# Three edits in a fused attention, MoE and routed-MoE kernel: one head first, dots by a count per step, a first gather without the last tile

## The chip, the cores and the metric

The kernel runs on one core of a Trainium2 chip. The core has five engines that each run their own queue of instructions: TensorE for matmuls (PE in the rows; PEld is its weight load), VectorE (DVE), ScalarE (ACT), GpSimd (POOL) and SyncE (SP), which here only issues transfers. Data lie in SBUF, matmul results in PSUM, inputs and outputs in HBM, and DMA engines move data between them. The metric is the time of one execution on the device in microseconds (us); lower is better.

## The reference

Three stages follow one another, each on the result of the one before. x has 1152 tokens of 512 numbers after the attention.

```python
def _attn_ref(q, k, v):                 # B 2, H 8, S 576, D 64
    q_rot, k_rot = (rotate(q), rotate(k))        # halves mixed with cos and sin of the position
    scores = scale * np.matmul(q_rot, k_rot.transpose(0, 1, 3, 2))
    scores = scores - np.max(scores, axis=-1, keepdims=True)
    attn = np.exp(scores)
    attn = attn / (np.sum(attn, axis=-1, keepdims=True) + 1e-09)
    return np.matmul(attn, v)

def _moe_ref(x, w_gate, w1, w2):        # N 1152, D 512, E 8, F 1024
    logits = x @ w_gate
    logits = logits - logits.max()
    P = np.exp(logits)
    for _ in range(8):
        P /= P.sum(1, keepdims=True) + 1e-09
        P /= P.sum(0, keepdims=True) + 1e-09
        P *= N / E
    for e in range(E):
        h = np.maximum(x @ w1[e], 0.0)
        out += P[:, e:e + 1] * (h @ w2[e])

def _moe2_ref(x, w_gate, w1, w2):       # same sizes, other weights
    logits = x @ w_gate
    order = np.argsort(-logits.flatten())
    for idx in order:                    # best pair of token and expert first
        tok, e = (int(idx) // E, int(idx) % E)
        if assigned[tok] >= 0 or counts[e] >= N // E:
            continue
        assigned[tok] = e
        counts[e] += 1
    for e in range(E):
        mask = assigned == e
        out[mask] = np.maximum(x[mask] @ w1[e], 0.0) @ w2[e]
```

## The kernel before

All matrices are fp32. Where a product needs full precision, an operand is split into a high part and a low part (ACT writes the high part, DVE or POOL subtracts it for the low part), and PE multiplies the parts.

**Attention** goes over 16 heads, two of them a pair P (variable g for the head; h is its place in the pair). For a pair, k and q are loaded (`load`, L1147), rotated (`prep_rot`, L1196, into `t1k` and `t1q`), split (`prep_hl`, L1211, into `hlk` and `hlq`) and transposed by PE (`tq`, L1242, into `khh`, `kll`, `qs`); v is split by `prep_v`. Then five tiles of scores per head follow: matmuls `S`, maximum, exponential, transposes of the result (`te`), product with v. Pair 0 is prepared ahead of the first score as a whole, both heads, and POOL rotates pair 1 meanwhile. What else falls into a head is placed by numbers: `at(2.9, ...)` puts a call behind 2.9 of its five tiles. Between them PE runs dummy matmuls (`warm`) at the start.

**The first MoE** (class Moe1) takes the experts one after the other; six of them by Strassen's scheme, expert 7 plainly in 24 steps (`step`, steps counted from K7). In each step PE makes a block of h, ACT writes its high part (L690), DVE its low part (L691), and the products with w2 add up in PSUM and are added to `acc` (nine tiles of 128 tokens). The gate of the second MoE is folded into this stage: its logits need 72 dot products (nine tiles by eight experts) of `acc` with the gate's columns `g2`, each one DVE instruction (`dot`, L966), and small matmuls (L1020, L1031) for what expert 7 adds. `plan` (L968) puts the dots into the steps: four a step from K7+3, three a step from K7+15. Weights come as raw tiles; `wconv` (L591) splits them, the low part on POOL (L607).

**The second MoE** (`moe2`) is written by a list scheduler (class Plan, L121): each operation has the operations it needs, an engine with an estimated duration, and a function; the planner emits them in order of estimated start, and PE's expert matmuls are its main line. For each expert a phase p picks tokens: `m` and its broadcast, compares (L229 to L232) on DVE, counts on PE (L241), `ok`, `a` and closing on DVE, the selection (`selb`, L297), its place (L302, L304), a one-hot matrix `hot` (L313), the row numbers (L320 on PE, `ix` L328 on DVE). With these POOL gathers the tokens' rows from `ysc` in HBM by two indirect transfers (L338, `xa` and `xb`), PE transposes them (L413, L414) and runs the matmuls of the expert (L422 with w1, L432 with w2, L441 back).

The seam is where the two stages meet. The last products of expert 7 for tiles 3 to 8 (the tail) fill PE while phase 0 picks its tokens. A finished tile of `acc` is written to `ysc` by `save` (L961) from SP's queue. The first gather waits for all saves, that of the last tile (8) among them. Behind the tail PE runs 24 dummy matmuls (`fill`, L484) until the gathered rows are there.

## Time and profile before

| | |
|---|---|
| Time, median of three runs | 1177.39 us (1174.03 to 1178.0) |
| Profiled execution, its own time | 1178.97 us |
| Its span (first to last instruction) | 1177.2 us |
| PE busy | 1148.8 us, 98% |
| DVE busy | 817.9 us, 69% |
| ACT busy | 421.4 us, 36% |
| POOL busy | 500.6 us, 43% |

One core's execution is shown. The profiled time lies 1.8 us above its span, and 1.6 us above the median. PE is nearly always busy, so the rows to read are the few in which it is not, and those in which what it does is a dummy: `warm` at the start, `fill` at the seam. In a row of the timeline the first number is the start in us, the second the length of the instruction (or of the group, with its count behind x), and the bracket at the end says how long the engine had been idle before it and what ended that. A wait for several things is put down to the one that came last.

### The profile page before, as it was taken

How to read it: one execution, taken by the hardware profiler on the slowest of the kernel's cores; microseconds unless marked ns; L12 is line 12 of the kernel's file. 1: busy time of each engine (PE TensorE's matmuls, PEld its weight loads, DVE VectorE, ACT ScalarE, POOL GpSimd, SP SyncE). 2: the span in 40 equal slices, each digit the busy share in tenths (PEclk: the TensorE clock that was granted, in tenths of full speed). 3: DMA queues.
4: the chain of work that ended last, by engine and by line, in shares of the span. 5: the costliest groups of instructions: out<-in, count | busy, mean ns of one | idle time of the engine just before them, and what ended most of it. 6: DMA issues, size and time to landing. Idle time of an engine off the chain costs nothing. (4 is left out here: it accounts for less than half of the span.)

```text
span 1177.2 us, 20269 instructions
## 1 busy us (share of the span) xinstructions
PE 1148.8 (98%) x7788; PEld 1029.8 (87%) x7791; DVE 817.9 (69%) x1785; ACT 421.4 (36%) x966; POOL 500.6 (43%) x460
## 2 busy tenths in 40 slices
PE   7999999999999999999999999999999999999997
PEld 4998988898888889888888889898989877899997
DVE  5999995256477777777777777666667888889200
ACT  4888886214322323232322232323322110222222
POOL 6787865405453434443453435433433000374111
PEclk9999999999999999999999999999999999999999
DMA  3223214200123222423233222111212003878830
GB/s 105 74 61 95 58 34 144 78 1 1 54 71 106 84 90 74 132 82 90 81 111 105 77 86 81 45 36 37 69 58 89 28 1 126 296 262 289 270 101 21
DMA packets 105247, 108.97 MB, mean 93 GB/s; under 512 B 27584, under 2 KB 68672, under 8 KB 105024
## 3 DMA queue, kind: packets, MB, share of 16 engines
q1 hardware_dynamic: 102816, 102.31, 28.0%
q0 software_dynamic: 2048, 4.72, 1.3%
q8 instruction: 61, 1.00, 0.4%
q10 hardware_dynamic: 288, 0.66, 0.2%
q14 instruction: 34, 0.28, 0.1%
HBM read 98.36 MB, written 4.72 MB: 88 GB/s over the span
## 5 line engine op out<-in xcount | busy, mean ns | idle before, releaser
L925 DVE SCALAR_TENSOR_TENSOR acc<-Y,pw,acc 128x512 f32<-128x512 f32 x216 | 158.5, 743 | 3.6 <-PE Y L923 2.6
L861 PE MATMUL T<-xH,wa 128*128 128x256 f32 (+1 forms) x576 | 137.6, 294 | 1.6 <-ACT v L881 1.3
L861 PEld LDWEIGHTS T<-big,wb 128*128 128x128 f32 x864 | 125.9, 188 | 12.6 <-DVE v L874 3.5
L861 PE MATMUL T<-big,wb 128*128 128x256 f32 (+1 forms) x864 | 133.9, 297 | 1.2 <-DVE v L874 1.2
L874 DVE TENSOR_TENSOR v<-T,v 128x256 f32<-128x256 f32 (+1 forms) x240 | 108.3, 451 | 37.4 <-PE T L861 34.5
L861 PEld LDWEIGHTS T<-xH,wa 128*128 128x128 f32 x576 | 99.9, 188 | 9.8 <-ACT v L881 4.1
L770 POOL TENSOR_TENSOR wa<-wraw,wa 128x512 fp32r<-128x512 f32 (+1 forms) x48 | 48.9, 1018 | 108.2 <-ACT wa L769 108.2
L682 PE MATMUL T<-xH,wa 128*128 128x384 f32 x336 | 92.7, 337 | 0.0
L867 ACT ACTIVATE hhA<-v 128x256 fp32r<-128x256 f32 x72 | 30.1, 418 | 152.6 <-DVE v L874 152.6
L861 PE MATMUL T<-xL,wa 128*128 128x256 f32 (+1 forms) x288 | 84.5, 293 | 0.0
L868 DVE SCALAR_TENSOR_TENSOR hlB<-v,hhB 128x320 fp32r<-128x320 f32 x72 | 56.9, 790 | 38.7 <-ACT hhB L867 38.7
L867 ACT ACTIVATE hhB<-v 128x320 fp32r<-128x320 f32 x72 | 34.0, 472 | 138.4 <-DVE v L874 138.4
L993 DVE SCALAR_TENSOR_TENSOR fr<-fr,fc 128x512 f32<-128x512 f32 x64 | 52.5, 820 | 34.4 <-DMA fr<-in_moe_w 34.4
L923 PE MATMUL Y<-wb,hhB 128*128 128x512 f32 x240 | 75.1, 394 | 0.0
L868 DVE SCALAR_TENSOR_TENSOR hlA<-v,hhA 128x256 fp32r<-128x256 f32 x72 | 50.6, 702 | 35.3 <-ACT hhA L867 35.3
L923 PE MATMUL Y<-wa,hhB 128*128 128x512 f32 x240 | 75.0, 394 | 0.0
L789 POOL TENSOR_TENSOR wb<-wraw,wb 128x512 fp32r<-128x512 f32 x24 | 30.6, 1297 | 103.4 <-ACT wb L788 103.4
L789 POOL TENSOR_TENSOR wa<-wraw,wa 128x512 fp32r<-128x512 f32 x24 | 30.6, 1297 | 99.9 <-ACT wa L788 99.9
L701 PE MATMUL Y<-wb,hh 128*128 128x512 f32 x216 | 69.0, 400 | 1.6 <-ACT acc L708 1.6
L1284 DVE TENSOR_REDUCE negmax<-S 128x1 f32<-128x576 f32 (+1 forms) x80 | 60.0, 751 | 6.8 <-PE S L1282 6.0
L682 PEld LDWEIGHTS T<-xH,wa 128*128 128x128 f32 x336 | 61.3, 188 | 2.0
L1288 ACT ACTIVATE big<-S,negmax 128x576 f32<-128x576 f32 (+1 forms) x80 | 59.0, 737 | 11.3 <-DVE negmax L1284 10.7
(294 smaller groups left out, 2995.6 us busy)
## 6 DMA issues: line engine op xcount, KB each, us to landing
wraw<-in_moe_w SPq DMA_DIRECT2D x52, 512.0 KB, 5.3
fr<-in_moe_w SPq DMA_DIRECT2D x64, 256.0 KB, 4.9
wraw<-in_moe_w SPq DMA_DIRECT2D x48, 256.0 KB, 3.2
big<-in_moe_w SPq DMA_DIRECT2D x20, 512.0 KB, 6.2
wa<-in_moe_w SPq DMA_DIRECT2D x18, 512.0 KB, 5.2
wb<-in_moe_w SPq DMA_DIRECT2D x14, 512.0 KB, 6.8
hlk<-hlk SPq DMA_DIRECT2D x14, 320.0 KB, 3.7
ysc<-acc SPq DMA_DIRECT2D x9, 256.0 KB, 2.1
```

Source lines behind the costliest of these rows:

```text
L682: nc.tensor.matmul(p[:, :CH], w[:, wi, kt, (fb % 2) * 128:(fb % 2) * 128 + 128], x[:, kt, o], start=(n == 0), stop=(n == 11))
L701: nc.tensor.matmul(self.Y[c][t], a[:, o], w[:, wi, fb % 2], start=(fb == 0 and n == 0), stop=(fb == FB - 1 and n == 2))
L789: G.tensor_tensor(d["W"][:, 1, h], r[:, 2 + h], d["W"][:, 0, h].bitcast(F32), op=OP.subtract)
L861: nc.tensor.matmul(bank[:, 0:n], d[t][:, ww, b, r * 128:(r + 1) * 128], x(xw, r), start=(first and i == 0), stop=(i == 5), skip_group_chec ...
L867: A.activation(HH[:, f, o], src, AF.Relu)
L868: V.scalar_tensor_tensor(HL[:, f, o], src, 0.0, HH[:, f, o].bitcast(F32), op0=OP.max, op1=OP.subtract)
L874: V.tensor_tensor(o, bank[:, 0:n], x, op=OP.add)
L923: nc.tensor.matmul(y, h[:, f, o], w[:, ww, f], start=(f == 0 and z == 0), stop=(f == 1 and z == 2))
L925: V.scalar_tensor_tensor(self.acc[:, t], y, self.pw[:, t, e:e + 1], self.acc[:, t], op0=OP.mult, op1=OP.add)
L993: nc.vector.scalar_tensor_tensor(r, r, 1.0, self.fc, op0=OP.mult, op1=OP.mult, accum_out=self.wf[:, f, e:e + 1])
L1284: nc.vector.tensor_reduce(m[0:n], p[0:n, :, :288], axis=AX.XY, op=OP.max, negate=True)
L1288: pexp.append(lambda: nc.scalar.activation(e[0:n, :576].rearrange("p (a c) -> p a c", a=2), p[0:n, :, :288], AF.Exp, bias=m[0:n], scale=1. ...
```

## The change

It has three parts.

**Attention.** Only head 0 is prepared ahead of the first score. `prep_rot` and `prep_hl` take a head of the pair as an argument, and `prep_rot` an engine. k of head 0 is rotated by DVE, q of head 0 by POOL; then POOL rotates k of head 1 and k of pair 1. q of head 1 is rotated by DVE within head 0, and its low parts and those of k's head 1 are made there. The loads are issued in that order, k and q have two raw buffers, the table of cosines and sines is loaded once and scaled for q by ACT. The split of k of pair 1 moves from 0.9 to 2.9 of head 0, behind v, the rotation of its q behind that, and the split of its q to 1.6 of head 1.

**Dots.** `plan` now has a list with the number of dots for each of the 24 steps of expert 7: from its first step on, five at most, two in the last five. The first ones go by gate columns that lie in tiles of the fold (`FC`) before `g2` is there. Six low parts of weights in the steps 0, 1 and 3 go to DVE instead of POOL.

**Seam.** The fills are gone. The first gather waits for the saves of tiles 3 to 7 only (they go by ACT's queue now), and the last tile's rows of `ysc` are zeroed beforehand (`zero`); their part of expert 0's input is added afterwards by four matmuls with the one-hot matrix and two additions on DVE (`late`). Behind the gathers of experts 0 and 1 POOL sets a word, which DVE copies (`tock`): DVE stops there until the gather is issued. The save of tile 8 goes behind the first gather.

The order in which POOL's instructions stand at the start of attention, before (names ending in k, q and v are those of k, q and v; `hlk` and `hlq` the low parts):

```order
L1205 TENSOR_TENSOR t_139<-rawq_95,tab 128x10x32
L1206 TENSOR_TENSOR t_139<-rawq_95,tab 128x10x32
L1205 TENSOR_TENSOR t_207<-rawk_96,tab 128x10x32
L1206 TENSOR_TENSOR t_207<-rawk_96,tab 128x10x32
L1208 TENSOR_TENSOR t1k<-rawk_96,tab 128x640
L1209 TENSOR_TENSOR t1k<-t1k,t_207 128x640
L1205 TENSOR_TENSOR t_213<-rawq_95,tab 128x10x32
L1206 TENSOR_TENSOR t_213<-rawq_95,tab 128x10x32
L1208 TENSOR_TENSOR t1q<-rawq_95,tab 128x640
L1209 TENSOR_TENSOR t1q<-t1q,t_213 128x640
L1222 TENSOR_TENSOR hlk<-t1k,hlk 128x10x64
L1234 TENSOR_TENSOR big_113<-rawv_97,zero 128x2x5x64
```

and after:

```order
L1243 TENSOR_TENSOR t2k<-rawk_97,tab 128x5x32
L1244 TENSOR_TENSOR t2k<-rawk_97,tab 128x5x32
L1248 TENSOR_TENSOR t1k<-rawk_97,tab 128x320
L1249 TENSOR_TENSOR t1k<-t1k,t2k 128x320
L1243 TENSOR_TENSOR t2k<-rawk_98,tab 128x10x32
L1244 TENSOR_TENSOR t2k<-rawk_98,tab 128x10x32
L1248 TENSOR_TENSOR t1k<-rawk_98,tab 128x640
L1249 TENSOR_TENSOR t1k<-t1k,t2k 128x640
L1278 TENSOR_TENSOR big_123<-rawv_99,zero 128x2x5x64
L1279 TENSOR_TENSOR big_123<-rawv_99,big_123 128x2x5x64
L1263 TENSOR_TENSOR hlk<-t1k,hlk 128x10x64
L1243 TENSOR_TENSOR t2q<-rawq_96,tab 128x10x32
```

Pieces of 320 (one head) stand ahead of pieces of 640, k of pair 1 stands before v, and q of pair 1 last, where it stood ahead of v.

DVE in the last steps of expert 7, before (L691 is the low part of h, L966 the dots):

```order
L966 SCALAR_TENSOR_TENSOR junk,lg<-acc,g_9447 128x512 x3
L691 SCALAR_TENSOR_TENSOR wraw<-T,wraw 128x384
L966 SCALAR_TENSOR_TENSOR junk,lg<-acc,g_9447 128x512 x3
L691 SCALAR_TENSOR_TENSOR wraw<-T,wraw 128x384
L966 SCALAR_TENSOR_TENSOR junk,lg<-acc,g_9447 128x512 x3
```

and after (L707 and L984):

```order
L707 SCALAR_TENSOR_TENSOR wraw<-T,wraw 128x384
L984 SCALAR_TENSOR_TENSOR junk,lg<-acc,g_9476 128x512 x2
L707 SCALAR_TENSOR_TENSOR wraw<-T,wraw 128x384
L984 SCALAR_TENSOR_TENSOR junk,lg<-acc,g_9476 128x512 x2
L707 SCALAR_TENSOR_TENSOR wraw<-T,wraw 128x384
L984 SCALAR_TENSOR_TENSOR junk,lg<-acc,g_9476 128x512 x2
L707 SCALAR_TENSOR_TENSOR wraw<-T,wraw 128x384
```

There are two dots between low parts where there were three.

DVE at the seam, before (the compares of phase 1; L710 adds tile 8):

```order
L229 TENSOR_SCALAR cmp<-mb,m 128x512
L231 TENSOR_SCALAR cmp<-mb,m 128x512
L232 SCALAR_TENSOR_TENSOR cmp<-mb,m,edge 128x128
L229 TENSOR_SCALAR cmp<-mb,m 128x640
L231 TENSOR_SCALAR cmp<-mb,m 128x384
L232 SCALAR_TENSOR_TENSOR cmp<-mb,m,edge 128x128
L710 SCALAR_TENSOR_TENSOR acc<-Y,pw,acc 128x512
```

and after (L341 is the copy that stops DVE; L726 adds tile 8):

```order
L231 TENSOR_SCALAR cmp<-mb,m 128x640
L232 SCALAR_TENSOR_TENSOR cmp<-mb,m,edge 128x128
L341 COPY tock<-tick 1x1
L726 SCALAR_TENSOR_TENSOR acc<-Y,pw,acc 128x512
L229 TENSOR_SCALAR cmp<-mb,m 128x512
L231 TENSOR_SCALAR cmp<-mb,m 128x512
```

The copy and the addition of tile 8 stand two compares (groups of three rows) earlier than that addition did, and the copy right ahead of it.

PE at the seam, from the sum of phase 1 (L256) to its placing (L302), before:

```order
L256 LDWEIGHTS ones_b
L256 MATMUL PV<-a,ones_b 128x72
L484 LDWEIGHTS ones_b
L484 MATMUL Y<-hot,ones_b 128x512
L484 LDWEIGHTS ones_b
L484 MATMUL Y<-hot,ones_b 128x512
L413 MATMUL Y<-ident,xa 128x72
L414 MATMUL Y<-ident,xb 128x72
L413 MATMUL Y<-ident,xa 128x72
L414 MATMUL Y<-ident,xb 128x72
L302 LDWEIGHTS bef_b
L302 MATMUL PV<-selb,bef_b 128x9
```

and after:

```order
L256 LDWEIGHTS ones_b
L256 MATMUL PV<-a,ones_b 128x72
L445 MATMUL Y<-xg,wa 128x144 x8
L302 LDWEIGHTS bef_b
L302 MATMUL PV<-selb,bef_b 128x9
```

Eight of expert 0's first matmuls (L445) now stand ahead of the placing of phase 1, and the transposes of the gathered rows stand earlier, outside this piece. Eight more stand between it and phase 1's index matmuls (L320), where there were two.

The diff, cut to its core:

```diff
             def gather():
...
+                xa = two.tile([HC, D], F32, name="xa")
+                xb = two.tile([HC, D], F32, name="xb")
...
-                if p == 0:
-                    G.memset(tick, 0)
+                if p < 2:
+                    t = tick if p == 0 else two.tile([1, 1], I32, name="tick1", bufs=1)
+                    G.memset(t, 0)
+                    V.tensor_copy(two.tile([1, 1], I32, name="tock"), t)
+
+            def zero():
+                z = two.tile([128, D], F32, name="zero", bufs=1)
+                G.memset(z, 0.0)
+                nc.sync.dma_start(ysc[(NT - 1) * 128:, :], z)
+
+            def hot_last():
+                d["hf"] = two.tile([128, CAP], F32, name="hotf", bufs=1)
+                nc.scalar.activation(d["hf"], d["hot"][:, NT - 1], AF.Copy)
...
-            op("ga", ["ad"] + ([("tin1", p - 2)] if p > 1 else []) + ([("ga", p - 1)] if p else [("save", t) for t in range(3, NT)]),
-               [("POOL", 2.1, 0.0), ("DMA", 0.9, 1.5 if p == 0 else 5.0)], gather)
+            op("ga", ["ad"] + ([("tin1", p - 2)] if p > 1 else []) + ([("ga", p - 1)] if p else ["zero"] + [("save", t) for t in range(3, NT - 1)]) +
+               ([("save", NT - 1)] if p == 1 else []),
+               [("POOL", 2.1, 0.0), ("DMA", 0.9, 5.0)] if p > 1 else [("DVE", 2.5, 0.0), ("DMA", 0.9, 5.0 if p else 1.0)], gather)
...
+            def late(h):
+                pt = m1.ybank()[:, 0:2 * CAP].rearrange("p (k c) -> p k c", k=2)
+                for k in range(2):
+                    o = slice((2 * h + k) * 128, (2 * h + k + 1) * 128)
+                    nc.tensor.matmul(pt[:, k], m1.acc[:, NT - 1, o], d["hf"], start=True, stop=True)
+                x = Z["xg", p][:, 2 * h:2 * h + 2]
+                V.tensor_tensor(x, pt, x, op=OP.add)
...
-        for i in range(CFG["FILL"]):
-            plan.add(("fill", i), [("spr", 0)], [("PE", 0.23, 0.0)], fill, main=True)
...
-        nc.gpsimd.tensor_tensor(l, r, h.bitcast(F32), op=OP.subtract)
+        (low or nc.gpsimd).tensor_tensor(l, r, h.bitcast(F32), op=OP.subtract)
...
-        self.nc.sync.dma_start(self.ysc[t * 128:(t + 1) * 128, :], self.acc[:, t])
+        (self.nc.sync if t < 3 else self.nc.scalar).dma_start(self.ysc[t * 128:(t + 1) * 128, :], self.acc[:, t])
...
-        put(k7 + 3, 4, [f for t in range(3, NT) for f in part(t, self.pl)])
+        p = [part(t, self.pl) for t in range(3, NT)]
+        dots = [q[e] for e in range(E) for q in p] + [f for t in range(3) for f in part(t, self.lg)]
+        for o, n in enumerate((1, 1, 4, 2, 4, 4, 5, 5, 3, 4, 4, 4, 3, 3, 3, 3, 3, 3, 3, 2, 2, 2, 2, 2)):
+            put(k7 + o, n, dots[:n])
+            dots = dots[n:]
         put(k7 + 9, 3, [lambda t=t: self.save(t) for t in range(3)])
-        put(k7 + 15, 3, [f for t in range(3) for f in part(t, self.lg)])
...
                 for part in range(2):
-                    self.wconv(x, part)
+                    self.wconv(x, part, low=self.nc.vector)
...
-        NR = 1
-        WARM = (8, 6, 3, 4, 3, 2, 2)
+        NR = {"q": 2, "k": 2, "v": 1}
+        WARM = (16, 3, 2, 4, 3, 2, 2)
...
-        load(0, "k")
-        nc.scalar.dma_start(tab[:, 1], rope[:, 1])
-        load(0, "q")
-        nc.scalar.dma_start(tab[:, 0], rope[:, 0])
+        nc.scalar.dma_start(tab[:, 1], rope)
+        for n in "kq":
+            load_h(0, n, 0)
+            load_r(0, n)
+        for n in "kq":
+            load_h(0, n, 1)
+        load(1, "k")
         load(0, "v")
+        load(1, "q")
+        nc.scalar.activation(tab[:, 0], tab[:, 1], AF.Copy, scale=0.125)
...
-        prep_rot(0, "k")
-        prep_rot(0, "q")
-        load(1, "kq")
-        prep_hl(0, "k")
-        prep_hl(0, "q")
+        prep_rot(0, "k", 0, nc.vector)
+        prep_rot(0, "q", 0)
+        prep_hl(0, "k", 0)
+        prep_rot(0, "k", 1)
+        prep_rot(1, "k")
+        prep_hl(0, "q", 0)
...
             if g == 0:
-                at(0.9, prep_hl, 1, "k")
-                at(0.9, load, 2, "kq")
+                at(0.02, prep_rot, 0, "q", 1, nc.vector)
+                at(0.9, prep_hl, 0, "k", 1)
+                at(1.3, prep_hl, 0, "q", 1)
                 at(1.9, prep_v, 0)
                 at(1.9, load, 1, "v")
-                at(2.9, prep_hl, 1, "q")
+                at(2.9, prep_hl, 1, "k")
+                at(2.91, prep_rot, 1, "q")
+                at(2.91, load, 2, "kq")
+            if g == 1:
+                at(1.6, prep_hl, 1, "q")
```

## Rows read from the trace of the kernel before

**Rows 1.** Page, part 2: busy tenths of PE in 40 slices.

```profile
PE   7999999999999999999999999999999999999997
```

**Rows 2.** Waits of PE: us in total, times, longest.

```profile
PE T L1242 <- ACT hlk L1227: 5.5, 1, 5.5
...
PE PV L1020 <- DVE wraw L691: 1.6, 1, 1.6
```

**Rows 3.** Timeline of PE in attention: start, length, operation, idle before.

```profile
18.00 1.04 PE L1280 MATMUL S<-khh,qs 128*128 128x288 f32 x2
...
35.71 0.60 PE L1242 MATMUL T<-ident,hlq 128*128 128x128 f32 x4
```

**Rows 4.** Timeline of DVE, start of attention.

```profile
6.32 0.49 DVE L1205 TENSOR_TENSOR t<-rawk,tab 128x320 f32<-128x320 f32 x1 [4.59 <-DMA rawk<-in_k]
...
12.60 1.48 DVE L1228 TENSOR_TENSOR hlk<-t1k,hlk 128x640 fp32r<-128x640 f32 x1
```

**Rows 5.** DMA issues of 0:9: count, KB each, median us to landing.

```profile
rawk<-in_k SPq DMA_DIRECT2D x2, 32.0 KB, 3.4
```

**Rows 6.** Timeline of POOL, start of attention.

```profile
14.77 2.12 POOL L1208 TENSOR_TENSOR t1k<-rawk,tab 128x640 f32<-128x640 f32 x1
...
18.57 0.85 POOL L1205 TENSOR_TENSOR t<-rawq,tab 128x320 f32<-128x320 f32 x1
...
21.84 1.55 POOL L1209 TENSOR_TENSOR t1q<-t1q,t 128x640 f32<-128x640 f32 x1
```

**Rows 7.** Timeline of ACT, head 0 of attention.

```profile
28.05 0.73 ACT L1221 ACTIVATE hlq<-t1q 128x640 fp32r<-128x640 f32 x1
```

**Rows 8.** Windows: length, busy us of PE, PEld, DVE, ACT, POOL; clock.

```profile
20.00:30.00 10.00, 9.31 (x68) 6.92 (x66) 7.71 (x13) 8.09 (x20) 8.71 (x7) 1.00 0.43 109
880.00:890.00 10.00, 10.00 (x53) 9.20 (x52) 1.87 (x3) 3.02 (x5) 5.06 (x3) 1.00 0.84 315
```

**Rows 9.** Timeline of DVE, late steps of expert 7.

```profile
946.54 0.68 DVE L966 SCALAR_TENSOR_TENSOR junk<-acc,g 128x512 f32<-128x512 f32 x1
...
961.66 0.55 DVE L691 SCALAR_TENSOR_TENSOR wraw<-T,wraw 128x384 fp32r<-128x384 f32 x1
```

**Rows 10.** Timeline of ACT, last step of expert 7.

```profile
959.78 0.49 ACT L690 ACTIVATE wraw<-T 128x384 fp32r<-128x384 f32 x1 [1.89 <-PE T L682]
```

**Rows 11.** Timeline of PE, end of expert 7.

```profile
962.27 0.34 PE L1020 MATMUL PV<-wraw,wfs 128*16 128x384 f32 x1 [1.60 <-DVE wraw L691]
...
964.92 2.15 PE L209 MATMUL T<-ident,m 128*128 128x128 f32 x9
```

**Rows 12.** Window behind the end of expert 7, columns as above.

```profile
964.00:970.00 6.00, 6.00 (x24) 4.99 (x24) 4.12 (x15) 1.47 (x3) 0.00 (x0) 0.72 0.00 0
```

**Rows 13.** Timeline of POOL at the seam: gathers of experts 0 and 1.

```profile
1001.07 1.15 POOL L338 DMA_INDIRECT xa<-ysc,ix  x1 [17.38 <-DVE cmp L229]
1002.52 0.96 POOL L338 DMA_INDIRECT xb<-ysc,ix  x1 [0.31 <-issue]
...
1012.63 6.88 POOL L338 DMA_INDIRECT xb<-ysc,ix  x1 [0.30 <-issue]
```

**Rows 14.** Timeline of DVE at the seam.

```profile
991.28 0.16 DVE L328 SCALAR_TENSOR_TENSOR ix<-idf 72x4 int32<-72x4 f32 x1
...
994.27 0.34 DVE L232 SCALAR_TENSOR_TENSOR cmp<-mb,m,edge 128x128 bf16<-128x128 f32 x1
...
997.29 0.75 DVE L710 SCALAR_TENSOR_TENSOR acc<-Y,pw,acc 128x512 f32<-128x512 f32 x1 [0.58 <-PE Y L701]
...
1005.11 0.18 DVE L297 CAST selb<-sel 128x9 bf16<-128x9 f32 x1
```

**Rows 15.** Page, part 6: the saves of acc to ysc.

```profile
ysc<-acc SPq DMA_DIRECT2D x9, 256.0 KB, 2.1
```

**Rows 16.** Timeline of PE at the seam.

```profile
1008.01 0.79 PE L320 MATMUL PV<-meta,hot 128*72 128x4 bf16 x18 [0.26 <-DVE hot L313]
```

**Rows 17.** Chain that ended last: h matmuls of a later expert.

```profile
1103.60 6.13 PE Y L422 x50
```

More of the change, by code (lines that the diff above doesn't have):

```diff
@@ L370, in phase @@
             if not last:
+                if p == 0:
+                    op("zero", [], [("POOL", 0.7, 0.1), ("SP", 0.1, 0.0), ("DMA", 0.9, 1.6)], zero)
+                    op("hf", ["spr"], [("ACT", 0.3, 0.1)], hot_last)
                 op("m", [("close", p - 1), ("left", p - 1)] + ([("at", p)] if p == 1 else []) if p else [], [("DVE", 0.5, 0.15)], prefer)
@@ L408, in tin @@
                 if h == 0:
-                    Z["xg", p] = X["p"].tile([128, KT, CAP], F32, name="xg")
+                    Z["xg", p] = two.tile([128, KT, CAP], F32, name="xg")
                 pt = m1.ybank()[:, 0:2 * CAP].rearrange("p (k c) -> p k c", k=2)
@@ L459, in expert @@
                    [("PE", 0.55, 0.2), ("ACT", 0.3, 0.15)], tin, h)
+            if p == 0:
+                for h in range(2):
+                    op(f"late{h}", ["hf", f"tin{h}", ("ev", NT - 1)], [("PE", 0.5, 0.2), ("DVE", 0.45, 0.1)], late, h)
             for f in range(FB):
@@ L477, in moe2 @@
                 plan.add(("ev", t), [("t", n)], [("DVE", 0.67, 0.1)], evac)
-                plan.add(("save", t), [("ev", t)], [("SP", 0.1, 0.0), ("DMA", 0.9, 1.6)], lambda t=t: m1.save(t))
-        X["f"] = None
-        def fill():
-            if X["f"] is None:
-                X["f"] = m1.ybank()
-            nc.tensor.matmul(X["f"], ones_b, S_[0]["hot"].rearrange("p t c -> p (t c)")[:, 0:512],
-                             start=True, stop=True)
-        for i in range(CFG["FILL"]):
-            plan.add(("fill", i), [("spr", 0)], [("PE", 0.23, 0.0)], fill, main=True)
+                plan.add(("save", t), [("ev", t)] + ([("ga", 0)] if t == NT - 1 else []), [("ACT", 0.3, 0.0), ("DMA", 0.9, 1.6)], lambda t=t: m1.save(t))
         nf = len(plan.line)
@@ L590, in wload, with wconv @@
         nc.sync.dma_start(r[:, 2:4], self.w2[e, f * 256:(f + 1) * 256, :].rearrange("(k p) c -> p k c", p=128))
-    def wconv(self, s, part, dve=False):
+    def wconv(self, s, part, dve=False, low=None):
         if s >= self.NS:
@@ L977, in part @@
         def part(t, dst):
-            return [lambda e=e: self.dot(dst[:, t, e:e + 1], self.acc[:, t], e) for e in range(E)]
+            return [lambda e=e: self.dot(dst[:, t, e:e + 1], self.acc[:, t], e, t >= 3 and e < 3) for e in range(E)]
         k7 = self.K7
         put(k7 + 1, 1, [self.fold_split])
-        put(k7 + 3, 4, [f for t in range(3, NT) for f in part(t, self.pl)])
+        p = [part(t, self.pl) for t in range(3, NT)]
[3 more added lines that the diff above has]
+            dots = dots[n:]
         put(k7 + 9, 3, [lambda t=t: self.save(t) for t in range(3)])
-        put(k7 + 15, 3, [f for t in range(3) for f in part(t, self.lg)])
     def fold_w(self, i):
@@ L995, in fold_w @@
             self.fold_col(e + 1)
+        if i == E * FB - 1:
+            self.FC = [self.fold_col(e, "fr" if e else "fc") for e in range(3)]
     def fold_raw(self, i):
@@ L1104, in rest @@
         self.sx.close()
+        self.fst.close()
     def tail(self):
@@ L1194, in attention, with prep_rot @@
         T1 = {}
[L1196 to L1199 removed]
+        def prep_rot(P, n, h=None, e=nc.gpsimd):
+            hs = slice(0, 2) if h is None else slice(h, h + 1)
+            nh = hs.stop - hs.start
+            x = raw[n][P % NR[n]][:, hs]
             ti = 0 if n == "q" else 1
[L1201 to L1210 removed]
@@ new lines, in prep_rot, with prep_hl @@
+            e.tensor_tensor(t2[:, :, :, 0:32], x[:, :, :, 32:64], nsin, op=OP.mult)
+            e.tensor_tensor(t2[:, :, :, 32:64], x[:, :, :, 0:32], sin, op=OP.mult)
+            if not h:
+                T1[n, P] = pone.tile([128, 2, 5, HD], F32, name="t1" + n, bufs=2 if n == "k" else 1)
+            t1 = T1[n, P][:, hs]
+            e.tensor_tensor(t1, x, cos, op=OP.mult)
+            e.tensor_tensor(t1, t1, t2, op=OP.add)
+        def prep_hl(P, n, h=None):
+            dup = 2 if n == "k" else 1
+            if not h:
+                HL[n, P] = ptwo.tile([128, 2, 5, 2, dup, HD], F32R, name="hl" + n)
+            hs = slice(0, 2) if h is None else slice(h, h + 1)
+            t1 = T1[n, P][:, hs]
+            hl = HL[n, P][:, hs]
```

115 lines of the change are left out of this document (54 added, 61 removed).

## Prediction

> **What bounds the kernel now.** I read the page's slices first: PE is busy for nine tenths or more of every slice but the first [rows 1]. So a change gains only what it takes out of PE's few waits, and a thing added on another engine costs only where PE comes to wait for it. The list of PE's waits comes next: the longest by far is one of 5.5 us at the start of attention, for k's high part, and one of 1.6 us stands at the end of expert 7, for the last low part that DVE makes [rows 2]. The timelines around these two and around the seam then say what ends each wait. At the start DVE waits until 6.32 us for the third of k's transfers [rows 4], and the first score matmul comes at 18.00 [rows 3]. At the end of expert 7 DVE is late by its own dots [rows 9]. At the seam the first gather begins only at 1001.07, behind the save of the last tile [rows 13], and PE runs the fill matmuls meanwhile: they are busy time on the page and no work, so the busy share hides this wait.
>
> **Attention.** Nothing of the arithmetic goes; head 0 alone stands ahead of the first score. DVE's start at 6.32 less the 3.4 us of such a transfer [rows 4, 5] puts k's third issue at 2.9 us, about 1.0 for each; k's head 0 now needs two of them, so DVE begins near 5.3. A 320-element operation took 0.49 there [rows 4]; the four halves are at most 4 x 0.49, and I take 1.6. q's head 0 goes wholly to POOL. There 320 elements took 0.85 and 640 took 1.55 [rows 6], so its halves are about 0.5 + 0.5 + 0.85 + 0.85 = 2.7 alone. Beside DVE the same 640 elements took 2.12, that is 1.37 times as much, 3.7. With a start near 6.0 it ends between 8.7 and 9.7; I take 9.2. Behind it come ACT's high part (0.73 for 640 elements [rows 7], half of that here) and DVE's low part (0.5 to 0.8), 1.1 together. In the kernel before, the last such low part ended near 15.6 (two operations of 1.48 from 12.60 [rows 4]), and the first score came 2.4 later [rows 3]. So now: 9.2 + 1.1 + 2.4 = 12.7, which is 5.3 earlier (4.8 to 5.8).
>
> Two things take this back. First, what was prepared ahead now lies within head 0: q's head 1 is four operations of DVE (1.6) and the low parts of head 1 three more (3 x 0.49), 3.1 together. In 20 to 30 us DVE was busy for 7.71 of 10 [rows 8], which leaves 2.3 free. If all the free time can be used the loss is 0.8, if none of it 3.1. I take 1.7, since PE, ACT and DVE take turns in head 0 and only some of the gaps lie where the work is ready. Second, POOL now does k of pair 1 and v first and rotates q of pair 1 last, behind its low part of k. ACT reached that place in head 0 10.05 behind the first score (28.05 less 18.00 [rows 3, 7]). From it the chain is ACT 0.73, POOL 1.55, rotation 4.8 (18.57 to the end of the operation at 21.84 [rows 6]), ACT 0.73, POOL 1.55: 19.4 us behind the first score. The transpose that needs it stood 17.7 behind (35.71 less 18.00 [rows 3]) and did not wait. It will now wait 1.7, and what is queued behind it on PE with it. What is left: 5.3 - 1.7 - 1.7 = 1.9 us. Best case 5.8 (neither loss); worst case 4.8 - 3.1 - 1.7 - 1.8 (the rotation at 1.37 times), a loss of 1.8.
>
> **Dots.** Their number stays 72. Late steps had three, and the last low part of DVE started at 961.66 [rows 9], while ACT's high part was done at 959.78 + 0.49 = 960.27 [rows 10]: DVE is 1.39 late, which is most of PE's wait of 1.60 [rows 11]. A dot costs 0.68 with its readout at about 0.73 pitch, a low part 0.55 [rows 9]. With two a step DVE needs 2.0 us per step, while two of ACT's high parts lie about 2.4 apart (0.49 plus the idle 1.89 [rows 10]), so no lag is left: 1.4 gained. The dots moved forward, and six low parts of weights taken from POOL, lie in steps where DVE was busy 1.87 us of 10 [rows 8]. Such a low part has 1024 elements; from 512 in 0.68 [rows 9] I take 1.4 each. The price is nothing as long as no step fills up. If DVE were as slow as beside POOL (640 elements in 1.48 [rows 4], 2.4 for 1024), the two ahead of the bank adds in the first step would hold PE by 2 us or so; but it is POOL's own work that has gone. Bounds: +0.6 to -1.6.
>
> The clock goes with this wait. In 964 to 970 the granted clock was 0.72 [rows 12], its lower level for part of that time, behind the stretch in which PE waited; that cost 0.28 x 6 = 1.7 us, and the transposes that DVE's compares wait for took 2.15 [rows 11]. With PE's idle time there cut by 1.4 I count 1.2 of it as gained (0 to 1.7).
>
> **Seam.** The first gather now needs tile 7's save, not tile 8's. DVE adds tile 7 right ahead of the indices, which are there at 991.44 [rows 14]. With 2.1 us for a save [rows 15], a little more behind 2 MB of weights, the gather starts at 993.4 to 994.6. Its two calls take 1.15 + 0.31 + 0.96 = 2.4 [rows 13], so the stopper that DVE reads is set near 996.4. DVE comes to it after its fourth compare, at 994.6 [rows 14], and stands 2.1 us. Two late adds come on top, 0.45 each (estimated from 512 elements in 0.68 [rows 9], for 288), and the old wait for tile 8's matmuls, 0.58 [rows 14], goes. 2.1 + 0.9 - 0.6 = 2.4: expert 1's selection, finished at 1005.29 before [rows 14], comes at 1007.7, and the index matmuls, 2.7 behind it before (1008.01 [rows 16]), start at 1010.4. By the order PE has then done 16 of expert 0's first matmuls, where it had done two. At 6.13 us for 50 [rows 17], 14 of them are 1.7 us. 2.4 - 1.7 = +0.7: the earlier gather is paid for by DVE's stop. Bounds: -1.5 (the gather done before DVE comes to the stopper) to +3 (0.6 more of waiting and the lower clock, 1.7).
>
> On the clock there: without the 24 fills PE has only counts, transposes and late matmuls until the first of the 16. I take no price for it, since those matmuls lie in time in which PE waits for DVE anyway; the case with a price is rival (d).
>
> **Sum.** -1.9 - 1.4 - 1.2 + 0.7 = -3.8 us. The profiled execution took 1178.97, so it would take 1175.2. It lay 1.6 above the median of the three runs, 1177.39, so the median comes to 1173.6.
>
> **Rivals.** (a) The start's lead stays whole: POOL is done in time and DVE finds room. For it speaks the 2.3 us of free DVE time [rows 8]; against it the 19.4 us chain. Attention then gives 5.3: -7.2, 1170.2. (b) POOL's chain takes the whole lead: the rotation runs at 1.37 times as it did at 14.77 [rows 6] and eats the remaining 1.9. Then -1.9, 1175.5, no change that can be seen. (c) Slower: the gather stays slow though DVE stops. Beside DVE's compares one call took 6.88 [rows 13]. If the first call, begun while compares still run, keeps that pace, the stopper is set 5.7 later, and DVE and then PE stand for that time: -3.8 + 5.7 = +1.9. The gather of expert 1 has a stopper too and would hold DVE another 5.7, while PE has some 16 first matmuls of expert 0 left (2.0 at 6.13 for 50 [rows 17]): 3.7 more, +5.6, 1183.0. It decides from a first call of 5 us on (1.15 + 3.8). Against it: the calls of 1.15 and 0.96 [rows 13] ran while DVE was idle or on small operations. The Trainium skill ("GPSIMD Engine Reference", Key points) says that GpSimd and VectorE share their memory interfaces, with contention beside VectorE instructions of certain kinds. The trace agrees with 6.88 beside compares and 0.96 beside small operations [rows 13]; by the rule a DVE that stands slows no gather.
>
> (d) The clock falls at the seam. With the fills gone PE's work there is sparse, as it was at the end of expert 7, where the clock fell and cost 1.7 [rows 12]. The same price here gives -3.8 + 1.7 = -2.1, 1175.3. Against it: most of a slow stretch would lie in DVE's shadow. The Trainium skill ("TensorE: Matmul & The Clock Gate", What's actually happening) says that the gate follows how busy PE has been lately; by it the fall is the likelier course. The trace agrees at the end of expert 7, and none of its stretches shows a seam without fills.
>
> **How the numbers follow.** Forecast 0.43 (own range 1171.3 to 1175.9), (a) 0.21, (b) 0.11, (d) 0.11, (c) 0.14. A measurement of this kernel can tell about 0.3% (3.5 us) from no change. The forecast lies just beyond that, so 0.27 of its 0.43 counts as faster and 0.16 as the same. Faster: 0.27 + 0.21 = 0.48; same: 0.16 + 0.11 + 0.11 = 0.38; slower: 0.14. The range for 8 in 10 reaches down past (a), with the clock's full price and a little of the seam, to 1167.5, and up into (c) to 1180.0.
>
> **What would show it.** First score near 12.7 us. The transpose of pair 1's q waiting on its low part for 1 to 2 us, some 34 us in: no wait there means (a), a first wait of 3 us or more means (b). At the end of expert 7, no wait of PE for DVE above 0.3 us, and a granted clock of 1.00 behind it. At the seam, a granted clock under 0.9 in the first 10 us behind the tail means (d). DVE's stop at the first stopper 1 to 3 us; both first calls of the gather about 1 us long: 5 us or more means (c). The forecast is wrong in its seam if expert 1's selection comes less than 1 us or more than 4 us later, counted from the indices of expert 0, than the 14.0 us of before (1005.29 less 991.28 [rows 14]), and wrong in its dots if PE waits in the first steps of expert 7.

## The result: slower by 0.56%

The changed kernel takes 1185.28 us (median of six, 1181.76 to 1186.02), the kernel before 1177.36 beside it: a ratio of 1.0056, 95% interval 1.004 to 1.0072. (The ratio compares all executions and is not the quotient of the two medians, which is 1.0067; the argument goes by the ratios.) The forecast was 1173.6, the range 1167.5 to 1180.0, so it was wrong in its sign. The profiled execution took 1185.45 us with a span of 1183.5 at a mean granted clock of 0.989. Each kernel has one trace, and executions differ: twelve of the kernels here have the old attention, and in nine of their traces the first score comes at 16.6 to 17.0 us and the transpose of pair 1's q at 33.7 to 34.1, while in three, the kernel before among them, they come at 17.8 to 18.0 and 35.5 to 35.7. So the traces below show mechanisms, and the ratios say what they cost.

### The profile page after: what moved, and what is told of

Its sections match the earlier page's. It is cut to its first block, busy times and chain, and to the rows that moved or that the text cites. A ratio compares the mean times of both kernels' runs of the same rounds, so it can differ in the third digit from the quotient of the medians.

```text
span 1183.5 us, 20257 instructions
## 1 busy us (share of the span) xinstructions
PE 1149.8 (97%) x7779; PEld 1032.9 (87%) x7779; DVE 825.8 (70%) x1800; ACT 423.7 (36%) x972; POOL 491.0 (41%) x464
## 3 DMA queue, kind: packets, MB, share of 16 engines
q1 hardware_dynamic: 101232, 101.46, 27.4%
## 5 line engine op out<-in xcount | busy, mean ns | idle before, releaser
L883 ACT ACTIVATE hhA<-v 128x256 fp32r<-128x256 f32 x72 | 30.1, 418 | 150.0 <-DVE v L890 150.0
```

The source lines that it names most:

```text
L883: A.activation(HH[:, f, o], src, AF.Relu)
```

## The profile after

PE's waits first (us in total, times, longest). The two that were named in the forecast are gone, and these two lead the list.

```profile
PE T L1286 <- ACT big L1332: 4.7, 2, 4.4
PE Y L425 <- DMA xa<-ysc,ix: 3.5, 1, 3.5
```

**Attention.** PE's timeline: the first score, the place where PE then stands, and the transpose of pair 1's q, which stood at 35.71 [rows 3].

```profile
12.53 0.53 PE L1324 MATMUL S<-khh,qs 128*128 128x288 f32 x2
...
22.67 1.11 PE L1286 MATMUL T<-ident,big 128*128 128x128 f32 x4 [4.35 <-ACT big L1332]
...
38.22 0.65 PE L1286 MATMUL T<-ident,hlq 128*128 128x128 f32 x4 [1.17 <-POOL hlq L1263]
```

The lead is there, 5.47 us at the first score, and by 38.22 it has become a lag of 2.5 behind the kernel before, and of some 4 behind the nine traces that began earlier. ACT's exponential, which PE waits 4.35 us for, waits in turn for a maximum on DVE. DVE's timeline shows what it did instead: the four operations that rotate q of head 1, here with three of the same sizes earlier.

```profile
4.92 0.33 DVE L1243 TENSOR_TENSOR t2k<-rawk,tab 128x160 f32<-128x160 f32 x1 [3.18 <-DMA rawk<-in_k]
...
5.39 0.48 DVE L1248 TENSOR_TENSOR t1k<-rawk,tab 128x320 f32<-128x320 f32 x1
5.91 0.49 DVE L1249 TENSOR_TENSOR t1k<-t1k,t2k 128x320 f32<-128x320 f32 x1
...
14.71 1.54 DVE L1243 TENSOR_TENSOR t2q<-rawq,tab 128x160 f32<-128x160 f32 x1
16.17 1.72 DVE L1244 TENSOR_TENSOR t2q<-rawq,tab 128x160 f32<-128x160 f32 x1
17.81 1.54 DVE L1248 TENSOR_TENSOR t1q<-rawq,tab 128x320 f32<-128x320 f32 x1
19.38 1.70 DVE L1249 TENSOR_TENSOR t1q<-t1q,t2q 128x320 f32<-128x320 f32 x1
21.01 0.75 DVE L1328 TENSOR_REDUCE negmax<-S 128x1 f32<-128x576 f32 x1
```

And POOL's in the same stretch:

```profile
14.53 1.54 POOL L1248 TENSOR_TENSOR t1k<-rawk,tab 128x640 f32<-128x640 f32 x1
16.15 1.56 POOL L1249 TENSOR_TENSOR t1k<-t1k,t2k 128x640 f32<-128x640 f32 x1
17.67 1.33 POOL L1278 TENSOR_TENSOR big<-rawv,zero 128x640 fp32r<-128x640 f32 x1
19.08 1.66 POOL L1279 TENSOR_TENSOR big<-rawv,big 128x640 fp32r<-128x640 f32 x1
```

Each of DVE's four ends a little behind the POOL operation beside it: the two of 160 elements 0.18 us behind (16.25 behind 16.07), the two of 320 elements 0.34 and 0.35 behind (21.08 behind 20.74). Together they last from 14.71 to 21.08, 6.4 us, where the same four on k of head 0, while POOL had nothing to do, lasted from 4.92 to 6.40, 1.5 us. The granted clock falls with PE's idle time, in the windows of 20 to 24 and 24 to 28 (columns as in rows 8), where all of 20 to 30 had 1.00 [rows 8]:

```profile
20.00:24.00 4.00, 1.33 (x6) 1.33 (x7) 4.00 (x7) 1.82 (x5) 0.74 (x1) 0.55 0.26 74
24.00:28.00 4.00, 4.00 (x21) 3.07 (x19) 2.86 (x5) 1.71 (x5) 0.00 (x0) 0.59 0.02 4
```

**Dots.** PE at the end of expert 7, against 1.60 and 2.15 in [rows 11]:

```profile
962.85 0.35 PE L1044 MATMUL PV<-wraw,wfs 128*16 128x384 f32 x1 [0.24 <-DVE wraw L707]
...
965.46 1.71 PE L209 MATMUL T<-ident,m 128*128 128x128 f32 x9
```

The wait is 0.24. The window behind it has a granted clock of 0.72, exactly as in [rows 12]:

```profile
964.00:970.00 6.00, 6.00 (x27) 5.01 (x28) 4.16 (x17) 1.47 (x3) 0.53 (x1) 0.72 0.11 44
```

**Seam.** The save of tile 7 (count, KB each, us from issue to landing) in the window of 991 to 993 after, and in that of 990 to 993 before; then the weights' issue on SP after:

```profile
ysc<-acc ACTq DMA_DIRECT2D x1, 256.0 KB, 5.2
```

```profile
ysc<-acc SPq DMA_DIRECT2D x1, 256.0 KB, 5.2
```

```profile
987.18 2.12 SPq L366 DMA_DIRECT2D wa<-in_moe_w  x4
```

The planner puts the weights behind the gather, but that sets only the place of their issue in SP's own queue. SP has nothing to wait for, so 2 MB stand in the DMA queues when ACT issues tile 7's save at 991.73, and it lands 5.2 us later. That is nothing new: in the kernel before, SP issued the weights from 986.61 on and tile 7's save at 991.21, and it took the same 5.2. The 2.1 of [rows 15] is the median of nine saves and hides this one. POOL and DVE at that place:

```profile
997.83 1.15 POOL L335 DMA_INDIRECT xa<-ysc,ix  x1 [13.68 <-DMA ysc<-acc]
999.29 0.96 POOL L335 DMA_INDIRECT xb<-ysc,ix  x1 [0.31 <-issue]
```

```profile
991.80 0.16 DVE L328 SCALAR_TENSOR_TENSOR ix<-idf 72x4 int32<-72x4 f32 x1
...
1000.37 0.14 DVE L341 COPY tock<-tick 1x1 int32<-1x1 int32 x1 [5.25 <-POOL tick L340]
...
1010.88 0.18 DVE L297 CAST selb<-sel 128x9 bf16<-128x9 f32 x1
```

The gather starts 0.9 us behind that landing and 6.0 us behind the indices, DVE stands 5.25 us at the stopper, and expert 1's selection comes 19.1 us behind the indices (13.8 before, 1005.11 less 991.28 [rows 14]; 14.0 to 15.6 in four other kernels with the old seam). PE:

```profile
1001.25 0.38 PE L425 MATMUL Y<-ident,xa 72*128 72x72 f32 x1 [3.47 <-DMA xa<-ysc,ix]
...
1009.01 4.18 PE L445 MATMUL Y<-xg,wa 128*128 128x144 f32 x16
...
1016.51 0.76 PE L320 MATMUL PV<-meta,hot 128*72 128x4 bf16 x18
...
1021.90 0.29 PE L455 MATMUL Y<-h,wa 128*128 128x144 f32 x1
```

The sixteen matmuls take 4.18, or 0.26 each; 50 took 6.13 before [rows 17], or 0.12. The windows of 18 us behind the tail, before and after, tell why (busy PE, PEld, DVE, ACT, POOL; clock):

```profile
997.20:1015.20 18.00, 16.11 (x198) 12.77 (x199) 15.52 (x52) 2.88 (x7) 6.74 (x6) 1.00 0.62 222
```

```profile
1002.00:1012.00 10.00, 7.91 (x82) 7.66 (x83) 8.67 (x34) 0.82 (x2) 0.32 (x1) 0.50 0.65 236
...
997.80:1015.80 18.00, 12.09 (x116) 11.54 (x117) 12.79 (x44) 2.49 (x6) 2.52 (x4) 0.62 0.60 208
```

From 1002 to 1012 the clock is at its lower level throughout (0.50, 1.2 GHz). Expert 0's first product with w2 comes 30.1 us behind the indices (1021.90 less 991.80) where it came 26.6 behind them (26.7 to 28.3 in the four others). From there to the end of the span it is 161.6 us, 159.3 before; where these further 2.2 are lost is left open.

## The experiments

Ratios are to the kernel before on the same chip, with their 95% interval. One theory was put on each part, with rivals named in the expectations.

**Each part alone.** Each of the first three has one part of the change and the rest as before.

```diff
+        prep_rot(0, "k", 0, nc.vector)
+        prep_rot(0, "q", 0)
...
+                at(0.02, prep_rot, 0, "q", 1, nc.vector)
```

> The kernel before with the attention part of the change alone. Lockstep theory: DVE's four operations on q of head 1 last about 1.5 us each because POOL's operations lie beside them, PE waits 4 us or more in head 0, and the whole is slower than before by 3 to 4 us, all of the change's loss up to the first MoE. Rival (the loss is the lower clock at 20 to 28 us that the missing warm matmuls bring): the same loss here, so this run only sizes it; the next one tells them apart. If the parts hang together, so that the loss needs the other two, this run is within 1 us of before.

```diff
-        put(k7 + 15, 3, [f for t in range(3) for f in part(t, self.lg)])
+            put(k7 + o, n, dots[:n])
```

> The kernel before with the dots' part alone (counts per step, early dots by gate columns, six low parts on DVE). Both theories: PE's wait for DVE's last low part falls from 1.60 to about 0.2, 1.4 to 2.0 us faster than before. Clock theory of the prediction: the granted clock behind expert 7 (964 to 970) stays at 1.00, another 1.2. Rival, by the changed kernel's trace: it falls to about 0.72 as before, so the gain ends at 2.0.

```diff
-        for i in range(CFG["FILL"]):
...
+                    V.tensor_copy(two.tile([1, 1], I32, name="tock"), t)
...
+        (self.nc.sync if t < 3 else self.nc.scalar).dma_start(self.ysc[t * 128:(t + 1) * 128, :], self.acc[:, t])
```

> The kernel before with the seam's part alone (first gather without the last tile, stoppers, no fills). Theory: the save of tile 7 lands about 6 us after its issue behind the 2 MB of weights, DVE stands about 5 us at the first stopper, the clock is at its lower level for about 13 us behind the tail, and the whole is 5 to 6 us slower than before. Rival (the seam loses only because the dots' part shifted it): within 1.5 us of before.

Attention alone 1.0040 (1.0019 to 1.0061), dots alone 0.9963 (0.9940 to 0.9985), seam alone 1.0024 (1.0003 to 1.0045). The seam costs half of what was expected of it. Dots and seam together:

> Dots and seam as in the change, attention as before. If the parts add up: 0.9963 times 1.0024, 0.1% faster than before (0.3% faster to 0.1% slower). If they depend on each other, as the whole with its attention mended suggests: 0.1% to 0.3% slower than before.

That is 0.9994 (0.9973 to 1.0015); the product of the two is 0.9987. All three multiply to 1.0027 against the whole's 1.0056 (1.004 to 1.0072); the intervals together allow it, and whether the parts also hurt each other is left open. With attention alone PE stands as in the whole change:

```profile
21.73 0.66 PE L1261 MATMUL T<-ident,big 128*128 128x128 f32 x4 [4.40 <-ACT big L1307]
...
37.73 0.66 PE L1261 MATMUL T<-ident,hlq 128*128 128x128 f32 x4 [1.05 <-POOL hlq L1238]
```

**Attention: q of head 1 rotated on POOL.** Only the engine and place of those four operations change, once with attention alone and once in the whole change.

```diff
         prep_rot(0, "k", 1)
+        prep_rot(0, "q", 1)
...
-                at(0.02, prep_rot, 0, "q", 1, nc.vector)
```

> The attention part alone, with q of head 1 rotated by POOL behind k of head 1 instead of by DVE within head 0. Lockstep theory: PE's wait of 4.35 us in head 0 goes, the low parts of head 1 on DVE may take up to 1.5 each while POOL works, POOL reaches the low part of pair 1's q near 35 us, and the whole is between 1.5 us faster and 1.5 us slower than before, at least 2 us faster than the attention part as it was. Rival (clock or loads): as slow as the attention part as it was, 3 to 4 us over before.

> The changed kernel with q of head 1 rotated by POOL, nothing else altered. Lockstep theory: 4 to 5 us of its 6.6 us loss go, 1 to 3 us slower than before. Rival (the parts depend on each other and the loss stays in the seam): under 2 us of it go.

Attention alone now has 0.9998 (0.9976 to 1.0020), the whole change 1.0015 (0.9999 to 1.0031), so 0.41%, about 4.8 us, of what the change loses hung on these four operations. In attention alone PE's wait in head 0 falls from 4.40 to 2.01, the clock stays, and q's transpose comes 5.4 earlier (3.8 in the whole change, 34.46 for 38.22):

```profile
19.82 0.63 PE L1261 MATMUL T<-ident,hlk 128*128 128x128 f32 x4 [2.01 <-DVE al L1342]
...
32.29 0.66 PE L1261 MATMUL T<-ident,hlq 128*128 128x128 f32 x4 [1.14 <-POOL hlq L1238]
```

```profile
20.00:24.00 4.00, 3.40 (x25) 2.43 (x23) 3.39 (x7) 2.58 (x7) 3.31 (x3) 1.00 0.02 6
```

The same trace tells which of DVE's operations are held. DVE, then POOL:

```profile
16.17 0.48 DVE L1238 TENSOR_TENSOR hlk<-t1k,hlk 128x320 fp32r<-128x320 f32 x1
16.58 1.83 DVE L1247 TENSOR_TENSOR hlk<-t1k,hlk 128x320 fp32r<-128x320 f32 x1
18.33 0.75 DVE L1303 TENSOR_REDUCE negmax<-S 128x1 f32<-128x576 f32 x1
...
20.07 0.68 DVE L1283 CAST khh<-T 128x512 fp32r<-128x512 f32 x1
```

```profile
16.27 1.79 POOL L1223 TENSOR_TENSOR t1k<-rawk,tab 128x640 f32<-128x640 f32 x1
18.14 1.66 POOL L1224 TENSOR_TENSOR t1k<-t1k,t2k 128x640 f32<-128x640 f32 x1
19.76 1.50 POOL L1253 TENSOR_TENSOR big<-rawv,zero 128x640 fp32r<-128x640 f32 x1
```

The same subtraction takes 0.48 when it starts ahead of POOL's operation, and 1.83, to the end of POOL's at 18.06 and a little more, when it starts behind. A reduction or a cast from PSUM beside POOL takes its usual 0.75 and 0.68. The 2.01 that PE still waits is for `al` (the low part of the exponentials), which stands in DVE's queue behind these two subtractions, the low parts of k's head 1: now they are held.

With the dots beside it:

> The dots' part and the attention part with q of head 1 on POOL, the seam as before. If the parts add up: 0.9963 times 0.9998, about 4 us faster than before (2 to 6). If the dots' gain rests on a lucky place of the clock: 1 to 2 us faster at most.

0.9972 (0.9954 to 0.9989), against 0.9963 for the dots alone: the mended attention adds nothing that can be measured. Here both subtractions start behind POOL's operations (at 16.25 and 17.90), and PE's wait behind them is a microsecond longer. DVE, then PE:

```profile
16.68 1.50 DVE L1247 TENSOR_TENSOR hlk<-t1k,hlk 128x320 fp32r<-128x320 f32 x1
18.09 1.81 DVE L1256 TENSOR_TENSOR hlk<-t1k,hlk 128x320 fp32r<-128x320 f32 x1
```

```profile
21.32 0.63 PE L1270 MATMUL T<-ident,hlk 128*128 128x128 f32 x4 [3.02 <-DVE al L1351]
```

The lead at the first score (4.94, 11.66 against 16.60) goes in three waits of PE: this one of 3.02 for DVE, 0.69 for ACT and 1.15 for POOL's low part of pair 1's q, 4.86 together, and the transpose of that q stands at 33.73, against 33.72. The whole change with q on POOL has the same 3.02, and there the clock was 0.50 from 22 to 25 as well.

**Seam, one suspect at a time.** Four kernels, each the seam alone with one edit. The fills back (24 dummy matmuls as before):

```diff
+        for i in range(24):
+            plan.add(("fill", i), [("spr", 0)], [("PE", 0.23, 0.0)], fill, main=True)
```

> The seam's part alone, with the 24 fill matmuls back. Clock theory: the granted clock stays at 1.00 behind the tail, expert 0's first matmuls run at 0.12 us each instead of 0.26, DVE's stop of 5.3 us and its chain stay as they are, and 2 to 4 us of the seam's loss go (within 1.5 us of before, or a little faster). Rival (DVE's stop is all that counts, PE's clock lies in its shadow): as slow as the seam part alone, within 1 us.

The saves of tiles 3 to 7 on SP, ahead of the weights:

```diff
-        (self.nc.sync if t < 3 else self.nc.scalar).dma_start(self.ysc[t * 128:(t + 1) * 128, :], self.acc[:, t])
+        (self.nc.sync if t < NT - 1 else self.nc.scalar).dma_start(self.ysc[t * 128:(t + 1) * 128, :], self.acc[:, t])
```

> The seam's part alone, with the saves of tiles 3 to 7 on SP's queue, so that the 2 MB of weights stand behind them. Queue theory (the save of tile 7 is late because the weights are already in the DMA queues): it lands about 2 us behind its issue instead of 5.3, the first gather starts 3 to 4 us earlier against the indices, DVE stands under 2 us at the first stopper, selection of expert 1 comes 3 us earlier, and 2 to 4 us of the loss go. Rival (the save is late for another reason, such as ACT's queue): the gather starts no earlier and the loss stays; or the weights, now later, hold PE's first matmuls instead (a wait for DMA there).

No stoppers:

```diff
-                    V.tensor_copy(two.tile([1, 1], I32, name="tock"), t)
```

> The seam's part alone, without the two stoppers. Theory (DVE's stop sets the phase-1 chain): DVE runs on, its compares are done 5 us earlier, but the gather's first call, beside compares, takes 5 us or more instead of 1.15, so the rows land 3 to 5 us later; the time is within 2 us of the seam part alone. Rival (the stop is the whole loss): 3 us or more faster than the seam part alone.

The planner told that the rows land later, so that PE's counts stand ahead of the rows' transposes:

```diff
-               [("POOL", 2.1, 0.0), ("DMA", 0.9, 5.0)] if p > 1 else [("DVE", 2.5, 0.0), ("DMA", 0.9, 5.0 if p else 1.0)], gather)
+               [("POOL", 2.1, 0.0), ("DMA", 0.9, 5.0)] if p > 1 else [("DVE", 2.5, 0.0), ("DMA", 0.9, 5.0 if p else 6.0)], gather)
```

> The seam's part alone, with the planner's latency for the first gather at 6.0 instead of 1.0 us, so that it puts both groups of counts of phase 1 ahead of the transposes of the gathered rows on PE. Order theory (PE stands in line for rows that come later than planned, and the counts behind them hold DVE's chain): the counts no longer wait for rows, selection of expert 1 comes within 17 us of expert 0's indices instead of 19.2, the time falls 2 to 4 us below the seam part alone. Rival (the stopper and the clock set the chain, not PE's order): within 1 us of the seam part alone.

In the table: the stop of DVE at the first stopper, then expert 1's selection and expert 0's first product with w2, both behind the indices, then the clock in the 18 us behind the tail.

| kernel | ratio (95%) | stop | selection | first w2 | clock |
|---|---|---|---|---|---|
| before | 1 | none | 13.8 | 26.6 | 1.00 |
| seam_only | 1.0024 (1.0003 to 1.0045) | 5.34 | 19.2 | 29.6 | 0.72 |
| seam_fills | 1.0028 (1.0015 to 1.0040) | 5.23 | 20.3 | 28.5 | 0.91 |
| seam_saves_first | 1.0063 (1.0040 to 1.0086) | 2.41 | 21.5 | 32.3 | 0.62 |
| seam_no_stop | 1.0035 (1.0019 to 1.0050) | none | 19.1 | 29.7 | 0.72 |
| seam_rows_late | 1.0113 (1.0077 to 1.0148) | 5.3 | 19.4 | 34.3 | 0.64 |
| seam_fills_no_stop | 1.0003 (0.9980 to 1.0027) | none | 19.1 | 27.4 | 1.00 |

Two other kernels with the changed seam, dots_seam and change_q1_pool, have a selection at 19.2 to 19.3, first w2 at 29.5 to 30.0 and a clock of 0.72; four with the old seam have 14.0 to 15.6, 26.7 to 28.3 and 0.91 to 1.00, so the row of before is the best of its kind. No single edit brings the seam back. The fills alone give back most of the clock (0.91) and 1.1 us of the first w2 product, and no time that can be measured (1.0028 against 1.0024), as the rival had it. With the saves first the gather starts 3.15 behind the indices and the stop is 2.41, as the forecast had it, but the rows now come late, since the weights' transfers are in the queues ahead of theirs (the DMA engines' busy share in the two us behind the call, 988 to 990, is 0.98; in the changed kernel, 998 to 1000, it is 0.13). POOL, then PE, of that kernel:

```profile
987.74 1.20 POOL L335 DMA_INDIRECT xa<-ysc,ix  x1 [10.80 <-DVE cmp L229]
```

```profile
995.81 0.38 PE L425 MATMUL Y<-ident,xa 72*128 72x72 f32 x1 [5.24 <-DMA xa<-ysc,ix]
```

The rows are there 8.1 us behind their call, 3.4 in the changed kernel. (The traced execution took 1180.21, the median of the four 1184.09.) Without the stopper DVE waits for PE instead (2.71 us for tile 8's product), and PE for the rows (3.16): the two waits hide each other, and the gather's calls are not the slow ones that were expected (1.15 and 1.14). Counts ahead of transposes are worse, but that edit is no test of their order alone: the later latency also put all of expert 0's first matmuls behind phase 1's index matmuls, where 32 of them stood ahead.

**Seam, two and three at a time.** Fills and no stopper; no stopper and rows late; fills and rows late; all three (the gather also counted on POOL in the planner); and that seam with the dots and the mended attention. The edits are those above.

> The seam's part with the fills back and without the stoppers, the rows' transposes early on PE as in the change. If stopper and fills are the pair (DVE runs on, PE keeps its clock): within 0.1% of the mended seam (0.14% slower than before). If PE's place for the rows still holds the counts: the counts of phase 1 wait behind the rows, selection of expert 1 stays 18 us or more behind the indices of expert 0, 0.25% to 0.4% slower than before.

> The seam's part without the stoppers and with PE's counts ahead of the rows, no fills. If stopper and place are the pair: selection of expert 1 at about 15 us behind the indices, and within 0.1% of the mended seam. If the clock matters beside them: selection early too, but PE at its lower level behind the tail for 8 us or more, 0.4% or more slower than before.

> The seam's part with the fills and PE's counts ahead of the rows, the stoppers kept. If the stopper alone sets DVE's chain once the rest is mended: selection of expert 1 at 19 us behind the indices, 0.3% or more slower than before; if not, within 0.1% of the mended seam.

> The seam's part with three edits: that later latency, no stoppers, the fills back. Order theory: DVE's chain runs as before the change (selection of expert 1 about 14 us behind the indices of expert 0), the gather's calls are slowed beside compares to 5 us or more, rows come no earlier than before, so the time is that of before within 2 us. Rival (the zeroing, late matmuls and additions cost by themselves): 3 us or more slower than before.

> All three parts, with q of head 1 on POOL and the mended seam. If the parts add up: dots and attention -3 us, seam -2 to +2: 1 to 5 us faster than before.

1.0003 (0.9980 to 1.0027), 1.0034 (1.0011 to 1.0057), 1.0070 (1.0043 to 1.0096), 1.0014 (0.9996 to 1.0032) and 0.9998 (0.9982 to 1.0014), in this order. Fills without a stopper is the only one of these seams whose clock stays whole. Its window of 18 us behind the tail, then the seam alone's:

```profile
994.00:1012.00 18.00, 15.79 (x173) 12.62 (x173) 13.89 (x46) 2.90 (x7) 2.76 (x4) 1.00 0.60 208
```

```profile
992.70:1010.70 18.00, 11.94 (x120) 11.51 (x121) 13.31 (x44) 2.49 (x6) 2.51 (x4) 0.72 0.62 206
```

Its selection is as late as in the seam alone (19.1), and still its first product with w2 comes 2.2 us earlier behind the indices. That speaks for the lower clock and PE's standing as the cost, and not for the late selection; but the intervals of the two ratios overlap, and the fills alone gave no time back, so what the seam's loss is made of is not shown. Nor does the clock alone rank these kernels: fills with rows late had 0.84 and lost 0.70%. That the fills hold the clock is plainer: over the 18 us behind the tail it is 0.81 to 1.00 in the ten kernels of this case with fills, and 0.62 to 0.72 in the eight without. None of the mended seams is faster than the seam before.

Two versions beat both kernels: the dots alone (0.9963, 1174.89 us) and the dots with the mended attention (0.9972, 1173.44 us). They can't be told apart.

## Why the prediction was wrong

**Attention (forecast -1.9, measured alone +0.40%, about +4.7).** The lead was right (5.3 forecast, 5.5 in the trace) and so was the chain behind k's part of pair 1 (9.4 forecast from ACT to PE, 38.22 less 28.59, or 9.6, in the trace). The step that failed is "q's head 1 is four operations of DVE (1.6)", with 3.1 as the most that head 0 could lose. They took 6.4, each held to the end of the POOL operation beside it, and PE stood 4.35 us with the clock down behind it. The row was in front of me: 640 elements at 1.48 beside POOL's 1.37 and 1.44 [rows 4], where 0.82 is what they take alone. DVE alone, then POOL beside DVE's 12.60, in the kernel before:

```profile
7.13 0.82 DVE L1208 TENSOR_TENSOR t1k<-rawk,tab 128x640 f32<-128x640 f32 x1
```

```profile
12.03 1.37 POOL L1205 TENSOR_TENSOR t<-rawk,tab 128x320 f32<-128x320 f32 x1 [0.94 <-DVE t1q L1209]
13.36 1.44 POOL L1206 TENSOR_TENSOR t<-rawk,tab 128x320 f32<-128x320 f32 x1
```

I read it as DVE being slower by a factor, used a factor for POOL, and used none for DVE in head 0. What these rows show is an operation that waits for POOL's end and then takes its own length: 640 elements end 0.68 behind it (14.08 behind 13.40), 320 elements 0.35, 160 elements 0.18. With the two engines in lockstep the cost is near a count of POOL's operations: 1.54 + 1.56 + 1.33 + 1.66 = 6.1.

The Trainium skill ("SBUF — State Buffer", SBUF: two separate sides) says that a VectorE operation with two SBUF inputs and a GpSimd operation that reads SBUF share a pair of ports under an exclusive lock: the one that starts first holds it for its whole instruction, and the other blocks. The trace agrees, with 1.54 and 1.72 for 160 elements beside POOL against 0.33 alone, and 0.75 for a reduction with one input.

**Dots (forecast -1.4, with the clock -2.6; measured alone -0.37%, about -4.3, between -1.8 and -7.1 by its interval; its median lies 2.0 under that of the kernel before).** The mechanism was right: the wait went from 1.60 to 0.24, and PE does not wait in expert 7's first steps. From the transpose of pair 1's q to the indices of expert 0 the traces have 951.3 us on average in the six kernels with this part and 953.8 in the twelve without, 2.5 less, though either kind spreads over 4 us and more.

**The clock behind expert 7 (forecast -1.2).** The step "the clock goes with this wait" held in three of the six traces without the wait. With the wait gone the clock still fell in the whole change (0.72 in 964 to 970), in the dots with the mended attention (0.57 in 958 to 962) and in all_mended (0.57 in 958 to 962), and did not fall in the dots alone, in dots_seam and in change_q1_pool (1.00). With the old wait of 1.60 it fell in eleven of twelve; not in the seam with the saves first (1.00 in 955 to 966). So the fall is commoner with the wait, and the wait does not decide it alone; what else does stays open.

**Seam (forecast +0.7, measured alone +0.24%, about +2.8).** Three steps failed. First "2.1 us for a save [rows 15], a little more behind 2 MB of weights": tile 7's save took 5.2, as it had behind the same weights in the kernel before, and the gather's call came 0.9 behind its landing, so the gather started 6.0 behind the indices instead of 2.0 to 3.2, and DVE's stop was 5.25 instead of 2.1. The row of that one save would have told; the median of nine did not. Second, "I take no price for it" for the clock: rival (d) came about, and where its 1.7 us was the price of six us at 0.72, here the clock was at 0.50 for ten, and below full from 1000 to 1014, and the sixteen matmuls took 0.26 each. What that costs in the whole time the fills did not show. Third, a reading error: [rows 17] counts 50 instructions, and a matmul that is one row of the program's order is two in the trace, so PE had 28 more first matmuls done, not 14. In the trace after, the selection is 5.3 later behind the indices (2.4 forecast), the index matmuls another 2.7 later behind it (none forecast), and from there to the first w2 product PE needs 4.5 less (1.7 forecast): 5.3 + 2.7 - 4.5 = 3.5. Against the four other traces of the old seam it is 1.8 to 3.4.

Measured alone, the three parts add up to +3.2 us of the whole's 6.6; whether the rest is noise or the parts' effect on each other is left open. Rival (c) had the right sign and nearly the size (1183.0), by luck, since its mechanism did not happen: the gather's calls took 1.15 and 0.96, and it was their start that was late. Rivals (a) and (b) fell: the whole lead went, but mostly to DVE and not to POOL's chain.

## What to carry to other kernels

Before work is moved to VectorE beside a busy GpSimd, look in the trace for an operation with two SBUF inputs that ends when GpSimd's does; if there is one, price the moved work by GpSimd's operations and not by its own size. Before a transfer is priced, read the row of that very transfer, and not the median of its kind. A transfer that a planner puts "behind" another is behind it only if its engine waits; look at what stands in the DMA queues when the urgent one is issued. And dummy matmuls that look like waste may hold the clock: taking them out is a trade against the slow stretch that follows. What that trade is worth in time these runs do not tell.
